# Hashed attention into a channel-mix layer: mu transposed in slot 5 of the first block, the third pair's turns and signs a slot down, natural loads ahead of the signs

## The chip, the cores and the metric

The kernel runs on one core of one Trainium2 chip. The metric is the time of one execution on the device in microseconds (us), the median over several runs. The engines are named as in the profile: PE is TensorE (matmul), PEld its weight load, DVE is VectorE, ACT is ScalarE, POOL is GpSimd, SP is SyncE, which issues most of the transfers; an engine's name with a q behind it (SPq, POOLq) is its queue of issues.

## The reference

The first half is attention in 32 heads (4 batches of 8, 768 tokens, 64 dimensions), in which a query sees only the keys of its own hash bucket. The bucket of a row is the six signs of its product with `proj`. The second half is a channel mix per batch: the attention output `x` is blended with itself shifted by one token, with the weights `mu_k` and `mu_r`, and goes through three matrices.

```python
q_bits = (np.einsum('bhsd,dk->bhsk', q, proj) > 0)      # k_bits likewise; proj is 64 x 6
mask = q_bucket[:, :, :, None] == k_bucket[:, :, None, :]
scores = np.where(mask, scale * np.matmul(q, k.transpose(0, 1, 3, 2)), -1e9)
attn_out = softmax(scores) @ v
...
xk = mu_k * x + (1.0 - mu_k) * x_prev                    # x: 4 x 768 x 512
xr = mu_r * x + (1.0 - mu_r) * x_prev
k = np.maximum(xk @ w_k, 0.0)                            # w_k: 512 x 1024
v = k * k @ w_v                                          # w_v: 1024 x 512
r = 1.0 / (1.0 + np.exp(-(xr @ w_r)))                    # w_r: 512 x 512
out = r * v
```

## The kernel before

The heads are taken two at a time, as 16 pairs `n` = 0 to 15, four to a batch. A pair has two heads `j` with six chunks of keys `jc` each, so twelve slots `s` = 0 to 11; slots are counted through as `G` = 12 n + s. The order in each engine's queue is written out by hand: the loop at L742 emits, slot by slot, everything that any engine does, and each engine works through its own queue in that order. Waits between engines follow from the data and from the buffers.

**A slot.** `score` (L445) makes one tile of scores, two matmuls of 70 rows: 64 dimensions and six signs. The signs are stored as plus and minus one half, so that a key of another bucket falls behind by a whole step, and ScalarE's exponential (L458, 128x768) turns that into nothing. Two score tiles can stand at a time. `pv` (L466) multiplies the exponentials of two slots earlier with the values; with the last chunk of a head VectorE takes the reciprocal and scales the output (L489, L490).

**Preparing a pair.** The operands `aq`, `ak` of a pair come out of four steps that are done during the pairs before it:
- `load_v` and `load_qk` (or, from pair 6 on, `load_blocks`) put the loads on SP's queue; `load_qk(n)` is two transfers of 384 KB and `load_v(n)` one. The line at L748 sets the slot.
- `turn(n, i, j, which, casts)` (L311) transposes q (i = 0) or k (i = 1) of head j in three fp32 transposes into a PSUM bank; VectorE copies that bank to SBUF (L330 for q, L332 for k), and two casts to bf16 bring its halves into `aq` or `ak` (L336, L337). The casts are done by GpSimd and VectorE, or both by GpSimd where `pool2` is given. The copied tiles `tq`, `tk` have one buffer each, a half for each head, and the next pair's go into the same.
- `bits(n, js, which)` (L403) multiplies the copied tiles with `projp` into a bank, VectorE takes the signs (`sg`, L413), and SP carries them into rows 64 to 69 of `aq` and `ak`: two small transfers (L418) per side and head, eight for a whole pair, the first head's ahead of the second's. `bits_direct` (L391) does the same for pair 0 without transfers.
- `values(n, j)` (L423) casts the values on GpSimd and adds them up over the chunks (two memsets, a cast, three additions).

**Behind a pair.** `turn_out(n)` (L497) transposes the output of a pair into a bank, VectorE copies it to `xt` (L504), and a shifted copy within `xt` (L508, L509) is made by GpSimd, or by VectorE in the fourth pair of a batch. `mix` (L514) needs the whole of `xt`: step 0 is the difference `df` (L521), step 1 the product with `mu_sb` (L525), step 2 the sum (L535), all on VectorE.

**Banks.** Besides the two score tiles there are four PSUM banks, A to D. In the first block (pairs 0 to 3) A and C collect the attention output of the two heads, and B and D serve all turns, signs, `turn_out` and the transposed mu; `misc_bank` gives B or D by slot. A bank is free again when VectorE has copied what stood in it.

**Mu.** `mu_k` and `mu_r` are loaded as eight rows (L698, L701), behind the loads of pairs 0 to 2 on SP's queue. TensorE transposes them into bank B and VectorE copies that to `mu_sb` (L770, L771), in slot 13; the first `mix` step that reads it stands in slot 19.

The order of the first 13 slots is the table `first_block` (L708). From pair 1 on general rules hold: signs of pair n+1 in slot 2, turns of pair n+2 in slots 4, 6, 8, 10, values of pair n+1 in slots 6 and 9 of the first block. The weights of the mix layer are loaded on GpSimd's queue in the slots of the table `weights` (L723). From pair 4 on the matmuls of the mix layer run between the attention slots, a share of them in every slot (`ffn`), with what is left behind pair 15.

Of the kernel before, what the change touches and what calls it, by code (L numbers as in the profile page):

```python
# [9 lines left out]
FP32 = mybir.dt.float32  # L10
# [6 lines left out]
P = 128  # L17
# [14 lines left out]
def kernel(  # L32
# [13 lines left out]
    nc = tc.nc  # L46
    B, H, S, D = q.shape
# [5 lines left out]
    NDC = DM // P  # L53
    NFC = DF // P
    NPB = H // 2
# [5 lines left out]
    ident32 = consts.tile([P, P], FP32, name="ident32")  # L61
# [13 lines left out]
    mu_rows = consts.tile([2 * NDC, P], FP32, name="mu_rows")  # L75
    mu_sb = consts.tile([P, 2 * NDC], FP32, name="mu_sb")
# [96 lines left out]
    def fast():  # L173
        with ExitStack() as fx:
# [4 lines left out]
            NKEEP = NPB + 2  # L179
# [21 lines left out]
            def bank(which, shape, dt, name):  # L201
                return bkp.tile(shape, dt, name=name, tag=f"bk{which}")
# [32 lines left out]
            def run_due():  # L235
                ready = sorted(x[:2] for x in due if x[0] <= clock[0])
                for key in ready:
                    fn = next(x for x in due if x[:2] == key)
                    due.remove(fn)
                    fn[2]()  # L240
# [70 lines left out]
            def turn(n, i, j, which, casts=None, copy=None):  # L311

                side = "qk"[i]
                au = augs[n % NSET]
                tp = bank(which, [P, HALF], FP32, f"tp{side}{n}_{j}")
                for c in range(3):
                    cols = slice(c * P, (c + 1) * P)
                    nc.tensor.transpose(tp[:, cols], nats[n][:, i, j, cols], ident32)  # L318
                if j == 0:
                    turned[n, side] = turnp.tile([P, S], FP32, name=f"t{side}{n}", tag=f"t{side}")  # L320
                dst = turned[n, side][:, j * HALF : (j + 1) * HALF]
                t32s[n, side, j] = dst
                if copy:
                    scale = 1.0 if side == "q" else ALPHA
                    nc.scalar.activation(dst, tp, AF.Copy, scale=scale)
                    nc.gpsimd.tensor_copy(au[side, j][0:D, 0:HALF], dst[0:D, :])
                    nc.scalar.activation(au[side, j][0:D, HALF:S], tp[D:P, :], AF.Copy, scale=scale)
                    return
                if side == "q":
                    nc.vector.tensor_copy(dst, tp)  # L330
                else:
                    nc.vector.tensor_scalar(  # L332
                        out=dst, in0=tp, scalar1=ALPHA, scalar2=None, op0=ALU.mult
                    )
                e0, e1 = casts or (nc.gpsimd, nc.vector)
                e0.tensor_copy(au[side, j][0:D, 0:HALF], dst[0:D, :])  # L336
                e1.tensor_copy(au[side, j][0:D, HALF:S], dst[D:P, :])  # L337
# [53 lines left out]
            def bits_direct(n, i, j, which):  # L391

                side = "qk"[i]
                bb = bank(which, [P, HALF], FP32, f"bd{side}{n}_{j}")
                nc.tensor.matmul(bb, projd, t32s[n, side, j], start=True, stop=True)
                for e in range(2):
                    nc.vector.tensor_scalar(
                        out=augs[n % NSET][side, j][D:AUG, e * HALF : (e + 1) * HALF],
                        in0=bb[D + 32 * e : D + 32 * e + NB, :],
                        scalar1=0.0, scalar2=0.5, op0=ALU.is_gt, op1=ALU.subtract,  # L400
                    )
# [285 lines left out]
            pool2 = (nc.gpsimd, nc.gpsimd)  # L687
            turn(0, 0, 0, "B", pool2)
            turn(0, 1, 0, "D", copy=True)
            for dst in (  # L690
# [13 lines left out]
            values(0, 0)  # L704
            turn(0, 0, 1, "B", pool2)
            turn(0, 1, 1, "D", pool2)

            first_block = {  # L708
                1: [lambda: bits_direct(0, 0, 1, "C")],
                2: [lambda: bits_direct(0, 1, 1, "B")],  # L710
                3: [lambda: turn(1, 0, 0, "D", pool2)],
                4: [lambda: turn(1, 1, 0, "C", pool2)],
                6: [lambda: bits(1, (0,), "B"), lambda: turn(1, 0, 1, "D")],
                8: [lambda: turn(1, 1, 1, "B")],
                9: [lambda: bits(1, (1,), "D"), lambda: turn(2, 0, 0, "B")],
                10: [lambda: turn(2, 1, 0, "D")],
                11: [lambda: turn(2, 0, 1, "B")],
                12: [lambda: turn(2, 1, 1, "D")],
            }


# [1 line left out]
            weights = {  # L723
                0: {10: ("k", 0, 2)},
                1: {6: ("k", 2, 2), 11: ("r", 0, 2)},
                2: {5: ("r", 2, 2), 9: ("v", 0, 4)},
                3: {2: ("v", 4, 4)},
            }
            LAG = 2
            MIXSLOT = 6  # L730
# [5 lines left out]
            def oo_bank(n, j):  # L736
                return "AC"[j] if n < NPB else "AB"[j]
# [4 lines left out]
            for G in range(nslots + LAG):  # L742
                clock[0] = G
                n, s = divmod(G, 12)
                live = G < nslots
                run_due()

                if live and s == (1 if n == 0 or n > NPB else 6 if n == NPB - 1 else 3):  # L748
                    if n < NPAIRS - 2:
                        load_v(n + 2)  # L750
                    if n + 3 < NPAIRS:
                        (load_qk if n + 3 < NKEEP else load_blocks)(n + 3)
                w = weights.get(n, {}).get(s)
                if w:
                    load_w(*w)
                old = chunks[G - LAG] if G >= LAG else None
                first = old is not None and old[2] == 0
                if live:
                    score(*chunks[G])
                if old and not first:  # L760
                    pv(*old, oo_bank(*old[:2]))
                rate = 25.9 / (NPB * 12 + (3 if n >= NPAIRS - NPB else 0))
                ffn(rate / 2)
                mb = misc_bank(n, s)
                if live:
                    for x in first_block.get(G, ()):
                        x()
                    if n == 1 and s == 1:
                        mups = bank("B", [P, 2 * NDC], FP32, "mups")
                        nc.tensor.transpose(mups, mu_rows, ident32[0 : 2 * NDC, 0 : 2 * NDC])  # L770
                        nc.vector.tensor_copy(mu_sb, mups)  # L771

                    if s == 2 and 1 <= n < NKEEP - 1:
                        bits(n + 1, (0, 1), "B")
                    if s == 10 and NKEEP <= n + 2 < NPAIRS:
                        bits_blocks(n + 2, "A")
                    if s == 3 and n >= 1:
                        turn_out(n - 1, mb)
                    if n >= NPB:
                        if s == 4 and n % NPB == 0:  # L780
                            mix((n - 1) // NPB, (n - 1) % NPB, 0)

                        if s in (8, 9) and n % NPB:
                            mix((n - 1) // NPB, (n - 1) % NPB, 0, [(0,), (1, 2)][s - 8])
                    ms = (5, 7, 9)
                    if s in ms and 1 <= n < NPB:
                        mix(0, n - 1, 0, [ms.index(s)])

                    xs = [NPB * 12 + x for x in (5, 10, 11, 12)]
                    if G in xs:  # L790
                        mix(0, xs.index(G), 1)
                    if n > NPB and s == (10 if n % NPB else 5):
                        mix((n - 1) // NPB, (n - 1) % NPB, 1)
                    if s in (4, 6, 8, 10) and 1 <= n < NKEEP - 2:
                        x = (s - 4) // 2
                        turn(n + 2, x % 2, x // 2, mb)
                    ts = (6, 7) if n % NPB == 0 else (4, 5)
                    if s in ts and NKEEP <= n + 2 < NPAIRS:
                        turn_blocks(n + 2, ts.index(s))
                    if n == 0 and s == 1:  # L800
                        values(0, 1)
                    vs_ = (8, 10) if n == 0 else (6, 9) if n < NPB else (0, 2)
                    if s in vs_ and n + 1 < NPAIRS:
                        values(n + 1, vs_.index(s))
                    if s in (8, 10) and NKEEP <= n + 2 < NPAIRS:
                        norm(n + 2, (s - 8) // 2)
                ffn(rate / 2)
                if old and first:
                    pv(*old, oo_bank(*old[:2]))
                if live and n >= NPB and n % NPB == 0 and s == MIXSLOT - 1:  # L810
                    queue.extend(ffn_items(n // NPB - 1))
# [14 lines left out]
            G = nslots + LAG  # L826
# [19 lines left out]
            x = 0  # L846
# [178 lines left out]
```

## Time and profile before

| | |
|---|---|
| median of 3 runs (lowest, highest) | 269.08 us (268.41, 269.61) |
| profiled execution: time, span | 269.2 us, 267.3 us |
| mean granted TensorE clock | 0.989 |
| busy: PE, ACT, DVE, POOL | 250.1, 216.0, 183.0, 121.2 us |
| ScalarE's exponentials, L458 | 192 of 909 ns, 167.4 us |
| ScalarE idle ahead of them | 24.1 us, 22.1 of it for scores |
| start of the scores of slots 14, 26, 38 | 22.99, 37.03, 47.55 us |

The span goes from the first to the last instruction; 1.9 us of the execution lie outside it. The 192 exponentials are one per slot. The profile's instructions carry the line of `kernel.py`, so the same line stands for all pairs; which pair an instruction belongs to is told from its order in time.

### The profile page before, as it was taken

Reading aid. Unit: us, or ns where it says so; the run is one execution under the profiler, and the core shown is the slowest. Engines: PE = TensorE matmul, PEld = TensorE weight load, DVE = VectorE, ACT = ScalarE, POOL = GpSimd, SP = SyncE. Lnnn points to the kernel's source line nnn. Section 1 sums busy time; section 2 is a strip of 40 time slices with the busy share of each in tenths; the row PEclk is TensorE's granted clock in tenths of the full one; section 3 lists DMA queues with packets and bytes.
Section 4 is the critical chain, followed back from the end, with each engine's and each line's share of the span. In section 5 each row is a group of like instructions: output and inputs, shape, how many; then the busy total and the mean of one; then the engine's idle time right before and its main releaser. Section 6 shows DMA issues by size and latency. Waiting matters only on the chain.

```text
span 267.3 us, 6634 instructions
## 1 busy us (share of the span) xinstructions
PE 250.1 (94%) x2441; PEld 151.6 (57%) x2441; DVE 183.0 (68%) x381; ACT 216.0 (81%) x320; POOL 121.2 (45%) x247
## 2 busy tenths in 40 slices
PE   7897999799999999999999999998999999989990
PEld 5564767465555655555565656564656665545450
DVE  2868578577899684759679586868596645775440
ACT  3576789888999998988999998989999988179700
POOL 3778478676768181822756293705483000000000
PEclk9999899999999999999999999999999999999998
DMA  7915195997769193977847291959520002220042
GB/s 227 369 57 83 14 259 98 237 207 160 170 122 241 36 221 63 205 195 192 209 127 155 63 214 22 234 173 242 146 60 6 3 2 82 78 78 0 14 151 86
DMA packets 26488, 35.41 MB, mean 132 GB/s; under 512 B 3064, under 2 KB 22992, under 8 KB 26448
## 3 DMA queue, kind: packets, MB, share of 16 engines
q1 hardware_dynamic: 23936, 31.89, 46.3%
q0 software_dynamic: 2144, 2.62, 6.4%
q8 instruction: 21, 0.34, 0.6%
q10 hardware_dynamic: 368, 0.39, 0.5%
q14 instruction: 19, 0.16, 0.2%
HBM read 30.68 MB, written 6.29 MB: 138 GB/s over the span
## 4 chain that ended last, share of the span: by engine, by line
PE 70%; DVE 10%; ACT 8%; DMA 5%; issue 2%; POOL 1%; SPq 0%; ACTq 0%; DVEq 0%
PE sc L451 16%; PE vp L553 15%; PE kp L553 12%; PE oo L478 9%; PE rp L553 7%; ACT pt L458 6%; DMA qk<-in_k_dram 3%; PE bb L369 2%; PE ot L503 2%; PE oo L469 2%; PE bb L409 2%; DMA vf<-in_v_dram 1%; DMA qk<-in_q_dram 1%; ACT sq L303 1%; PE tpq L318 1%
## 5 line engine op out<-in xcount | busy, mean ns | idle before, releaser
L458 ACT ACTIVATE pt<-sc,expb 128x768 bf16<-128x768 f32 x192 | 167.4, 909 | 24.1 <-PE sc L451 22.1
L451 PE MATMUL sc<-aq,ak 70*128 70x384 bf16 x384 | 94.5, 327 | 1.8 <-ACT pt L458 0.5
L478 PEld LDWEIGHTS <-pt 128*128 128x128 bf16 x1152 | 61.0, 98 | 26.8 <-issue 1.1
L478 PE MATMUL oo<-va,pt 128*128 128x65 bf16 x1152 | 66.9, 194 | 0.0
L553 PE MATMUL kp<-xk,wk_sb 128*128 128x384 bf16 x256 | 55.7, 326 | 2.6 <-DVE kr L578 1.1
L553 PE MATMUL vp<-wv_sb,k 128*128 128x512 bf16 (+1 forms) x200 | 51.9, 371 | 0.0
L451 PEld LDWEIGHTS <-ak 70*128 70x128 bf16 x384 | 35.2, 98 | 26.2 <-issue 5.1
L586 DVE TENSOR_TENSOR k<-kr 128x384 bf16<-128x384 bf16 x64 | 26.7, 433 | 6.4 <-ACT kr L576 5.9
L553 PEld LDWEIGHTS <-wk_sb 128*128 128x128 bf16 x256 | 21.7, 97 | 14.2 <-issue 4.0
L553 PE MATMUL rp<-wr_sb,xr 128*128 128x512 bf16 x96 | 28.9, 379 | 0.1
L353 POOL CAST aq<-tq 64x768 bf16<-64x768 f32 x20 | 16.5, 823 | 26.6 <-PE sc L451 11.9
L509 POOL COPY xt<-xt 128x127 bf16<-128x127 bf16 x12 | 3.5, 293 | 48.5 <-DVE xt L504 48.5
L576 ACT ACTIVATE kr<-kp 128x384 bf16<-128x384 f32 x36 | 18.1, 503 | 7.8 <-PE kp L553 7.8
L553 PEld LDWEIGHTS <-k 128*128 128x128 bf16 x200 | 16.8, 97 | 12.8 <-issue 2.7
L439 POOL TENSOR_TENSOR s<-vf 128x192 f32<-128x192 f32 x32 | 22.0, 688 | 0.0
L618 DVE SCALAR_TENSOR_TENSOR os<-th,vp 128x512 f32<-128x512 bf16 (+1 forms) x25 | 16.5, 662 | 7.2 <-PE vp L553 6.0
L489 DVE RECIPROCAL rc<-oo 128x6 f32<-128x6 f32 x32 | 6.1, 190 | 21.8 <-PE oo L478 21.8
L504 DVE COPY xt<-ot 128x768 bf16<-128x768 bf16 x16 | 8.9, 558 | 17.2 <-PE ot L503 17.0
L578 DVE TENSOR_SCALAR kr<-kp 128x384 bf16<-128x384 f32 x28 | 15.4, 552 | 6.9 <-PE kp L553 6.6
L490 DVE TENSOR_TENSOR ob<-oo,rc 128x384 bf16<-128x384 f32 x32 | 17.8, 558 | 1.1
L355 POOL TENSOR_SCALAR ak<-tk 64x768 bf16<-64x768 f32 x20 | 16.6, 832 | 2.8 <-DVE tk L343 1.3
L303 ACT ACTIVATE sq<-blk 128x768 bf16<-128x768 f32 x20 | 17.1, 853 | 0.0
(83 smaller groups left out, 305.8 us busy)
## 6 DMA issues: line engine op xcount, KB each, us to landing
blk<-in_q_dram SPq DMA_DIRECT2D x40, 176.0 KB
blk<-in_k_dram SPq DMA_DIRECT2D x40, 176.0 KB
vf<-in_v_dram SPq DMA_DIRECT2D x16, 384.0 KB
out_dram<-os SPq DMA_DIRECT2D x23, 256.0 KB
qk<-in_q_dram SPq DMA_DIRECT2D x5, 384.0 KB
qk<-in_k_dram SPq DMA_DIRECT2D x5, 384.0 KB
wk_sb<-in_moe_w_k_dram POOLq DMA_DIRECT2D x2, 512.0 KB, 5.6
wv_sb<-in_moe_w_v_dram POOLq DMA_DIRECT2D x2, 512.0 KB, 8.8
```

Source lines behind the costliest of these rows:

```text
L303: nc.scalar.activation(junk.rearrange("p (u d) -> p u d", u=NTOK), blks[n][:, i, :, 0:32], AF.Square, scale=1.5, accum_out=nrm[:, i, n : n ...
L353: eng.tensor_copy(dst, src)
L355: eng.tensor_scalar(out=dst, in0=src, scalar1=ALPHA, scalar2=1.0, op0=ALU.mult, op1=ALU.mult,)
L439: nc.gpsimd.tensor_add(s3, vf[:, 0 : 3 * D], vf[:, 3 * D : 6 * D])
L451: nc.tensor.matmul(sc[:, sp, 0:HALF], au["k", j][:, jc * P : (jc + 1) * P], au["q", j][:, sp * HALF : (sp + 1) * HALF], start=True, stop=True,
L458: nc.scalar.activation(pt.rearrange("p (s q) -> p s q", s=2), sc[:, :, 0:HALF], AF.Exp, bias=expb, scale=SCALE,)
L478: nc.tensor.matmul(oo[:, ic, :], pts[n, j, jc][:, ic * P : (ic + 1) * P], vas[n, j][:, jc, :], start=False, stop=(jc == NC_ - 1 and ic == ...
L490: nc.vector.tensor_tensor(out=obs[n][:, :, j * D : (j + 1) * D], in0=oo[:, :, 0:D], in1=rc.to_broadcast([P, NC_, D]), op=ALU.mult,)
L553: nc.tensor.matmul(box["t"], lhs(), rhs(), start=(i == 0), stop=(i == len(mms) - 1))
L576: nc.scalar.activation(kr, kp, AF.Relu, scale=HALFROOT)
L586: lambda: nc.vector.tensor_tensor(out=k2, in0=kr, in1=kr, op=ALU.mult),
L618: nc.vector.scalar_tensor_tensor(out=os_, in0=mx["th", b, c][:, ms], scalar=1.0, in1=vp, op0=ALU.add, op1=ALU.mult,)
```

## The change

- The transposed mu moves from slot 13 to slot 5, still in bank B.
- In block 0 no slot has two entries any more: the turn of pair 1's second q goes from slot 6 to 7, and the four turns of pair 2 from slots 9 to 12 to slots 10 to 13. Their casts, one of two on VectorE before, are both done by GpSimd.
- The signs of pair 2 go from slot 14 to 15, and the turns of pair 3 from slots 16, 18, 20, 22 to slots 17, 19, 21, 23, in the same banks as before. (The text's "third pair" is pair 2.)
- The natural loads of pairs 1 and 2 (`load_v` of pairs 3 and 4, `load_qk` of pairs 4 and 5) go from slot 3 of the pair to slot 1, on SP's queue ahead of that pair's eight sign transfers and not behind them.
- The second half of `w_r` is loaded in slot 4 of pair 2, not 5, and the second half of `w_v` in slot 0 of pair 3, not 2.

```diff
+            def transpose_mu():
+                mups = bank("B", [P, 2 * NDC], FP32, "mups")
+                nc.tensor.transpose(mups, mu_rows, ident32[0 : 2 * NDC, 0 : 2 * NDC])
+                nc.vector.tensor_copy(mu_sb, mups)
             first_block = {
...
-                6: [lambda: bits(1, (0,), "B"), lambda: turn(1, 0, 1, "D")],
-                8: [lambda: turn(1, 1, 1, "B")],
-                9: [lambda: bits(1, (1,), "D"), lambda: turn(2, 0, 0, "B")],
-                10: [lambda: turn(2, 1, 0, "D")],
-                11: [lambda: turn(2, 0, 1, "B")],
-                12: [lambda: turn(2, 1, 1, "D")],
...
+                5: transpose_mu,
+                6: lambda: bits(1, (0,), "B"),
+                7: lambda: turn(1, 0, 1, "D"),
+                8: lambda: turn(1, 1, 1, "B"),
+                9: lambda: bits(1, (1,), "D"),
+                10: lambda: turn(2, 0, 0, "B", pool2),
+                11: lambda: turn(2, 1, 0, "D", pool2),
+                12: lambda: turn(2, 0, 1, "B", pool2),
+                13: lambda: turn(2, 1, 1, "D", pool2),
             }
...
-                2: {5: ("r", 2, 2), 9: ("v", 0, 4)},
-                3: {2: ("v", 4, 4)},
+                2: {4: ("r", 2, 2), 9: ("v", 0, 4)},
+                3: {0: ("v", 4, 4)},
...
-                if live and s == (1 if n == 0 or n > NPB else 6 if n == NPB - 1 else 3):
+                if live and s == (6 if n == NPB - 1 else 3 if n == NPB else 1):
                     if n < NPAIRS - 2:
                         load_v(n + 2)
                     if n + 3 < NPAIRS:
...
-                    if n == 1 and s == 1:
-                        mups = bank("B", [P, 2 * NDC], FP32, "mups")
-                        nc.tensor.transpose(mups, mu_rows, ident32[0 : 2 * NDC, 0 : 2 * NDC])
-                        nc.vector.tensor_copy(mu_sb, mups)
-
-                    if s == 2 and 1 <= n < NKEEP - 1:
+                    if s == (3 if n == 1 else 2) and 1 <= n < NKEEP - 1:
                         bits(n + 1, (0, 1), "B")
...
-                    if s in (4, 6, 8, 10) and 1 <= n < NKEEP - 2:
-                        x = (s - 4) // 2
+                    tn = (5, 7, 9, 11) if n == 1 else (4, 6, 8, 10)
+                    if s in tn and 1 <= n < NKEEP - 2:
+                        x = tn.index(s)
                         turn(n + 2, x % 2, x // 2, mb)
```

More of the change, by code (lines that the diff above doesn't have):

```diff
@@ L706, in fast @@
             turn(0, 1, 1, "D", pool2)
+            def transpose_mu():
+                mups = bank("B", [P, 2 * NDC], FP32, "mups")
+                nc.tensor.transpose(mups, mu_rows, ident32[0 : 2 * NDC, 0 : 2 * NDC])
+                nc.vector.tensor_copy(mu_sb, mups)
             first_block = {
[L709 to L712, printed above, removed]
-                6: [lambda: bits(1, (0,), "B"), lambda: turn(1, 0, 1, "D")],
-                8: [lambda: turn(1, 1, 1, "B")],
-                9: [lambda: bits(1, (1,), "D"), lambda: turn(2, 0, 0, "B")],
-                10: [lambda: turn(2, 1, 0, "D")],
-                11: [lambda: turn(2, 0, 1, "B")],
-                12: [lambda: turn(2, 1, 1, "D")],
+                1: lambda: bits_direct(0, 0, 1, "C"),
+                2: lambda: bits_direct(0, 1, 1, "B"),
+                3: lambda: turn(1, 0, 0, "D", pool2),
+                4: lambda: turn(1, 1, 0, "C", pool2),
+                5: transpose_mu,
[7 more added lines that the diff above has]
+                13: lambda: turn(2, 1, 1, "D", pool2),
             }
@@ L765, in fast @@
                 if live:
-                    for x in first_block.get(G, ()):
-                        x()
-                    if n == 1 and s == 1:
-                        mups = bank("B", [P, 2 * NDC], FP32, "mups")
-                        nc.tensor.transpose(mups, mu_rows, ident32[0 : 2 * NDC, 0 : 2 * NDC])
-                        nc.vector.tensor_copy(mu_sb, mups)
-                    if s == 2 and 1 <= n < NKEEP - 1:
+                    if G in first_block:
+                        first_block[G]()
+                    if s == (3 if n == 1 else 2) and 1 <= n < NKEEP - 1:
                         bits(n + 1, (0, 1), "B")
```

## The prediction, made before the result was known

> **What bounds the kernel now.** I read the page first (ScalarE 81% busy, TensorE 94%, and a chain that is 70% TensorE over the whole span), then ScalarE's row of the timeline over the first five pairs of heads, where the diff works. A slot is one score tile and one 128x768 exponential, so every gap in this row is lost time. The columns are start, duration, engine and line, operation, count, and in brackets the idle time before.
>
> ```profile
> 12.51 3.44 ACT L458 ACTIVATE pt<-sc,expb 128x768 bf16<-128x768 f32 x4 [0.42 <-PE sc L451]
> 16.68 2.48 ACT L458 ACTIVATE pt<-sc,expb 128x768 bf16<-128x768 f32 x3 [0.73 <-PE sc L451]
> 20.20 4.30 ACT L458 ACTIVATE pt<-sc,expb 128x768 bf16<-128x768 f32 x5 [1.04 <-PE sc L451]
> 27.81 0.90 ACT L458 ACTIVATE pt<-sc,expb 128x768 bf16<-128x768 f32 x1 [3.31 <-PE sc L451]
> 29.43 9.13 ACT L458 ACTIVATE pt<-sc,expb 128x768 bf16<-128x768 f32 x11 [0.71 <-PE sc L451]
> 39.17 9.90 ACT L458 ACTIVATE pt<-sc,expb 128x768 bf16<-128x768 f32 x12 [0.62 <-PE sc L451]
> 49.69 3.41 ACT L458 ACTIVATE pt<-sc,expb 128x768 bf16<-128x768 f32 x4 [0.62 <-PE sc L451]
> 54.56 6.47 ACT L458 ACTIVATE pt<-sc,expb 128x768 bf16<-128x768 f32 x8 [1.46 <-PE sc L451]
> ```
>
> Between the gaps ScalarE never rests: 9.13 us for 11 tiles is 0.83 us a slot. In slots 6 to 42 the gaps sum to 0.73 + 1.04 + 3.31 + 0.71 + 0.62 + 0.62 + 1.46 = 8.49 us. Two are large. For the first I read the timeline of VectorE and TensorE.
>
> ```profile
> 22.30 1.37 DVE L337 CAST aq<-tq 64x384 bf16<-64x384 f32 x1
> ...
> 25.14 0.16 DVE L771 COPY mu_sb<-mups 128x8 f32<-128x8 f32 x1
> ...
> 25.35 0.51 PE L409 MATMUL bb<-tq,projp 128*32 128x384 f32 x1 [1.86 <-DVE mu_sb L771]
> ```
>
> The transposed mu (22.83, slot 13) sits in bank B until VectorE copies it out at 25.14, and VectorE is late: it still has copies and casts of pair 2 to do, one of them stretched from 0.35 to 1.37 us beside GpSimd's work. The sign products of pair 2 (slot 14) want bank B, so TensorE stands. The wait is paid twice: in the windows of 1 us the granted clock (the column after the five engines) falls to half behind it.
>
> ```profile
> 25.00:26.00 1.00, 0.65 (x8) 0.16 (x8) 0.29 (x2) 0.00 (x0) 1.00 (x4) 0.98 1.14 212
> 26.00:27.00 1.00, 1.00 (x12) 0.59 (x9) 0.56 (x1) 0.00 (x0) 0.03 (x1) 0.50 0.49 90
> 27.00:28.00 1.00, 1.00 (x12) 0.65 (x10) 0.00 (x0) 0.19 (x1) 0.00 (x0) 0.50 0.00 0
> ```
>
> The second large gap is in the chain of waits: pair 5's k, issued behind eight sign transfers, lands at 53.48, and its transpose waits 1.45 us.
>
> ```profile
> 45.89 7.59 DMA qk<-in_k_dram
> 53.48 0.14 issue
> 53.61 0.52 PE tpk L318 x3
> ```
>
> **The change, part by part.** The sum is made against the profiled execution: 269.2 us, its span of 267.3 and 1.9 around it; the median, 269.08, is 0.1 lower.
>
> Mu in slot 5. It adds a 0.22 us transpose and a 0.16 us copy there and removes both from slot 13. TensorE gets to it at 14.40. Ahead of the mu loads on SP's queue stand eight loads of 384 KB, 3.15 MB; the rates of the 1 us windows sum to 3.1 MB by 11.0, and even the loads behind mu are through by 14.3. So mu is there; were it not, the wait would be about 1 us at most. Behind the transpose stand the score of slot 6 and the sign products in B, which wait for a copy that ends near 14.9 and start at 15.07 instead of 15.01: nothing lost. In slot 6 the 0.48 us turn no longer stands between the signs and the score of slot 7, so the gap of 0.73 becomes about 0.35.
>
> Turns of pairs 1 and 2 a slot down. In slot 9 the sign products wait for the k copy of slot 8. VectorE now runs q copy and cast behind reciprocal and product of the last output (0.22 + 0.48 + 0.58 + 0.30 from 16.5, k copy to 18.65), so the products end near 19.6 rather than 19.30, but the turn of 0.48 behind them is gone. The score of slot 10 comes at 19.95 rather than 20.11. With ScalarE's queue emptied at 18.80, that gap is 1.25 instead of 1.04, and its next tile starts at 20.05.
>
> Casts on GpSimd. VectorE loses four casts (0.42, 0.41, 1.37, 0.35 us) in slots 9 to 13, GpSimd gains four at 0.55 (14.02, 14.57, 15.14: start to start). So VectorE keeps up: the turns of slots 10 to 13 then cost TensorE 0.35 beside 0.51 for score and output, hidden under 0.83. The k copy of slot 13 ends near 24.15; the sign products of slot 15 start near 24.5 with nothing in their way. The 3.31 is gone. But products (0.78) and output transposes (0.35) now share slot 15, so the score of slot 16 comes near 25.7 and the 0.71 stays as about 0.75. That tile starts at 26.1 instead of 29.43: 3.3 us gained here (5.79 of gaps become 2.35).
>
> GpSimd's queue is the price. Before, it had 3.32 us to spare:
>
> ```profile
> 25.49 0.50 POOL L336 CAST ak<-tk 64x384 bf16<-64x384 f32 x1
> 25.94 0.09 POOL L508 MEMSET xt<- 128x1 bf16 x1
> 29.35 0.29 POOL L509 COPY xt<-xt 128x127 bf16<-128x127 bf16 x1 [3.32 <-DVE xt L504]
> ```
>
> After, from the second cast of pair 1 done at 19.4: value sums 1.87, weight issue 0.94, casts 1.1, value sums 1.9, six casts 3.3, set and copy 0.4, so the shifted copy of the first output tile ends at 28.8, where VectorE writes that tile at 26.3. The mix difference (L521), now in slot 17 ahead of the turn in VectorE's queue, waits until 28.85, 2 us behind its slot. From there to the last k copy of pair 3 VectorE needs the 5.4 us it took from 31.03 to 36.43, and one q copy and cast more (0.95), which stood ahead of the difference before: 35.0 or so. The sign products of slot 26 would start at 34.0 and now at 34.8 to 35.0. The gap there grows from 0.62 to about 1.4: 0.8 lost. That is my least sure term: 0 if GpSimd runs 0.8 sooner, 1.6 if 0.8 later. I take 0.8, the sum of its rows. Value sums of pair 2 end near 33.7, ahead of their use at 35.6.
>
> Loads ahead of the signs. In pairs 1 and 2 the loads move from slot 3 to slot 1, past eight sign issues of 0.68. Pair 5's k then goes out near 34.5 instead of 45.89, and the turn that waited for it comes near 50: the 1.46 goes, and ScalarE, full up to 53.10, has nothing else late there. What the signs pay, by the nearest rows: pair 4's 1.18 MB, issued 32.64 to 34.20 with a weight load of as much time beside it, was through by 39.5, the windows show. The same load from 23.3 is through by 28.5; the first head's four signs, issued 25.4 to 28.1, land near 30, and slot 24 wants them at 32. In pair 2: issued to 38.6, wanted near 43.9. Nothing, from below; the bound from above is a rival.
>
> Weights. Two GpSimd issues (0.71 and 0.78) a slot or two sooner pass one cast that waits for VectorE anyway; hidden in idle times of 1.36 and 0.65 there.
>
> Sum: 3.3 (rounded down from 5.79 - 2.35 = 3.4) - 0.8 + 1.5 = 4.0; 269.2 - 4.0 = 265.2, and 0.1 less for the median: 265.1. Behind 62 us nothing moves in slots, and every later stage starts sooner by the same.
>
> **The rivals.** One: the queue costs nothing. The difference also waits less if GpSimd's value sums run undisturbed, and 0.8 comes back: 264.3; were slot 10's gap of 1.25 to vanish as well, 263.0. For it: VectorE makes fewer casts against GpSimd. Against: the sum above is of undisturbed rows already.
>
> Two: the loads bring little. Weight loads near 40 to 50 us may hold up something else, and the 1.46 stays: 266.6. Against it are the 11 us by which the load goes out sooner.
>
> Three: GpSimd is later still. Its casts take 0.69 to 0.74 beside a cast on VectorE, not 0.50. If the stretch to 28.8 grows by 2 us, TensorE waits 2.8 before slot 26 and the clock halves again, as it did after 1.86: 2 for the wait and about 0.7 for the gap behind it, 267.8. The trace bears this price out: 1.86 us of wait gave the clock of 0.50, 1.45 us at 53.6 did not. The Trainium skill (TensorE: Matmul & The Clock Gate, Part 1) has the clock fall only after an idle window of about 3.4 us; by that rule 0.7 falls away, but the trace halved it after less.
>
> Four, on the slower side: the signs starve behind the loads. A sign transfer put on SP's queue after 1.18 MB lands with the rest of it. Where the loads drain as slowly as pair 5's k did (7.59 us from issue, with weight loads beside it), signs issued at 28.1 land at 35.7 and slot 24 waits 3.6; in slot 36 (38.6 + 7.6 = 46.2 against 43.9) 2.3 more. With 0.7 for the clock twice that is 7.3 against a gain of 4.0: 272.4. It begins to cost when a sign takes over 4 us to land, and makes the kernel slower when both together pass 4.0. Against it: a weight load ran beside pair 4's load too, and 5.2 us sufficed for both. The Trainium skill (DMA: Bandwidth & Descriptors, Queues, rings and completion order) says that each DMA engine takes one queue's descriptors in ring order and changes between queues by packets. By that rule signs do wait for the loads, and its time would be that of this rival if weights took half the engines; no row of before shows a sign behind a load.
>
> That the change does not act as said hardly can be: the wait of slot 14 is one on bank B.
>
> **How the numbers follow.** Forecast 0.50 (264.3 to 266.3); rival one 0.19, two 0.12, three 0.12, four 0.07. A measurement of this kernel can tell about 0.5%, 1.35 us, from no change. Forecast, one and two are faster, and half of three: 0.87; the other half, near 267.8 and above, is the same: 0.06; four is slower: 0.07. The range from 262.9 to 268.3 leaves out rival four, the worst of three, and a little below.
>
> **What would show it.** Right: no ScalarE gap over 1.5 us from 12 to 60 us, clock 1.00 throughout, the eleventh tile of pair 1 no later than 33 us, a GpSimd xt copy near 28.8 with VectorE's L521 waiting for it, no wait for qk in pair 3. Wrong: a wait of scores for aq or ak from a DMA at slots 24 or 36 (rival four), a TensorE wait over 1.8 us for VectorE at slot 26 (three), a wait for mu_rows in slot 5.

## The result and the profile after

The changed kernel takes 266.39 us (median of 6 runs, 265.33 to 266.69), the kernel before in the same session 268.75 (6 runs): a ratio of 0.9903, 95% interval 0.9875 to 0.9931, so 2.6 us faster (0.0097 of 268.75; 1.9 to 3.4); the two medians differ by 2.4. The forecast was 265.1. In the table of the experiments the ratios leave out runs that lie over 1.5% above the fastest of their kernel and the medians do not, which matters for one kernel there, loads_back. The profiled execution took 266.43 with a span of 264.6, against 269.2 and 267.3 before.

ScalarE's row of the timeline, for the stretch shown of before:

```profile
13.63 3.48 ACT L458 ACTIVATE pt<-sc,expb 128x768 bf16<-128x768 f32 x4 [0.42 <-PE sc L451]
17.58 2.78 ACT L458 ACTIVATE pt<-sc,expb 128x768 bf16<-128x768 f32 x3 [0.48 <-PE sc L451]
21.23 5.17 ACT L458 ACTIVATE pt<-sc,expb 128x768 bf16<-128x768 f32 x6 [0.87 <-PE sc L451]
27.13 6.64 ACT L458 ACTIVATE pt<-sc,expb 128x768 bf16<-128x768 f32 x8 [0.72 <-PE sc L451]
34.14 2.48 ACT L458 ACTIVATE pt<-sc,expb 128x768 bf16<-128x768 f32 x3 [0.38 <-PE sc L451]
37.59 9.90 ACT L458 ACTIVATE pt<-sc,expb 128x768 bf16<-128x768 f32 x12 [0.97 <-PE sc L451]
48.11 9.90 ACT L458 ACTIVATE pt<-sc,expb 128x768 bf16<-128x768 f32 x12 [0.62 <-PE sc L451]
```

The 3.31 and the 1.46 are gone: ahead of slots 7 to 43 the gaps sum to 0.48 + 0.87 + 0.72 + 0.38 + 0.97 + 0.62 = 4.04 us against 8.49. A gap of 0.38 ahead of slot 24 is new, and the 0.62 ahead of slot 27 has become 0.97. What the forecast named as the cause stands in VectorE's row and in GpSimd's, and the run xt_vector below tests it:

```profile
26.83 0.55 DVE L504 COPY xt<-ot 128x768 bf16<-128x768 bf16 x1
30.02 0.56 DVE L521 TENSOR_TENSOR df<-xt 128x768 bf16<-128x768 bf16 x1 [2.64 <-POOL xt L509]
```

```profile
29.09 0.50 POOL L337 CAST ak<-tk 64x384 bf16<-64x384 f32 x1
29.54 0.10 POOL L508 MEMSET xt<- 128x1 bf16 x1
29.70 0.29 POOL L509 COPY xt<-xt 128x127 bf16<-128x127 bf16 x1
```

Where GpSimd waited 3.32 us for the output tile before, VectorE now waits 2.64 us for GpSimd. And everything stands about 1.1 us late against the working of the forecast. There are 4.4 us fewer gaps, but the span is only 2.7 us shorter: of the difference 1.1 went ahead of the first tile, 0.3 behind the last one, and the rest within the stretches between the gaps. Two pieces of the chain of waits (start, duration, what), of before and of after:

```profile
6.04 0.90 PE bdq L395 x2
```

```profile
6.30 1.62 PE bdq L395 x2
7.92 1.29 PE bdk L395 x2
```

The same two products take 0.90 and 1.62 us. The trace's record of the granted clock begins with full clock at 5.48 us before and at 9.44 after; the first tile starts at 9.38 and 10.46. The stream of instructions up to there is the same in both.

### The profile page after: what moved, and what is told of

It reads as the page before. It is cut to its first block, busy times and chain, and to the rows that moved or that the text cites. A ratio compares the mean times of both kernels' runs of the same rounds, so it can differ in the third digit from the quotient of the medians.

```text
span 264.6 us, 6633 instructions
## 1 busy us (share of the span) xinstructions
PE 250.3 (95%) x2441; PEld 151.5 (57%) x2441; DVE 180.0 (68%) x377; ACT 216.1 (82%) x320; POOL 123.0 (46%) x251
## 4 chain that ended last, share of the span: by engine, by line
PE 72%; ACT 9%; DVE 7%; POOL 4%; DMA 2%; issue 2%; SPq 0%; ACTq 0%; DVEq 0%; POOLq 0%
PE sc L451 17%; PE vp L553 15%; PE kp L553 14%; PE oo L478 9%; ACT pt L458 8%; PE rp L553 7%; PE bb L369 3%; PE oo L469 2%; PE ot L503 2%; PE bb L409 1%; DMA vf<-in_v_dram 1%; DMA qk<-in_q_dram 1%; PE bdq L395 1%; DVE ob L490 1%; DVE kr L578 1%
## 5 line engine op out<-in xcount | busy, mean ns | idle before, releaser
L553 PE MATMUL rp<-wr_sb,xr 128*128 128x512 bf16 x96 | 28.9, 379 | 0.1
L439 POOL TENSOR_TENSOR s<-vf 128x192 f32<-128x192 f32 x32 | 22.7, 708 | 0.0
```

Of the source, the lines that this page charges most:

```text
L439: nc.gpsimd.tensor_add(s3, vf[:, 0 : 3 * D], vf[:, 3 * D : 6 * D])
L553: nc.tensor.matmul(box["t"], lhs(), rhs(), start=(i == 0), stop=(i == len(mms) - 1))
```

## The experiments

To keep the start apart from the rest, I read the start of each slot's tile in ScalarE's row, take it from the first tile of the same execution, and subtract the same difference of the kernel before. So -3.38 in column "slot 16" means that the work from slot 0 to slot 16 took 3.38 us less than before. One execution of each kernel was profiled. The first six columns of numbers are of that execution, the median is of the timed runs. In the same comparisons the kernel before had medians of 268.75 (changed), 269.21 (the next four kernels of the table), 268.77 (the next three, and before_again) and 269.50 (the last three).

| kernel | full clock at | first tile | slot 16 | slot 28 | slot 44 | last tile | median us | ratio to before (95%) |
|---|---|---|---|---|---|---|---|---|
| before | 5.48 | 9.38 | 0 | 0 | 0 | 0 | 268.75 | |
| before_again | 9.66 | 10.43 | 0.01 | -0.07 | -1.20 | -1.15 | 269.11 (one) | |
| changed | 9.44 | 10.46 | -3.38 | -2.66 | -4.25 | -4.02 | 266.39 | 0.9903 (0.9875 to 0.9931) |
| loads_alone | 4.42 | 9.32 | +0.59 | +1.30 | -0.27 | 0.00 | 268.82 | 0.9976 (0.9951 to 1.0001) |
| mu_alone | 10.23 | 10.77 | -2.84 | -2.91 | -4.01 | -4.18 | 266.31 | 0.9899 (0.9862 to 0.9935) |
| split_casts | 9.39 | 10.35 | -2.11 | -2.36 | -3.94 | -3.61 | 266.06 | 0.9884 (0.9852 to 0.9916) |
| xt_vector | 4.60 | 9.39 | -3.38 | -3.52 | -5.10 | -4.72 | 265.02 | 0.9855 (0.9823 to 0.9887) |
| loads_back | 9.46 | 10.30 | -3.45 | -2.72 | -3.19 | -2.99 | 267.27 | 0.9924 (0.9890 to 0.9957) |
| fill | 5.61 | 9.68 | -3.39 | -2.67 | -4.25 | -3.89 | 265.86 | 0.9886 (0.9856 to 0.9916) |
| fill_xt | 3.86 | 9.22 | -3.38 | -3.51 | -5.09 | -3.72 | 264.73 | 0.9847 (0.9815 to 0.9878) |
| late_wv | 5.34 | 9.44 | -3.38 | -2.65 | -4.24 | +1.54 | 271.47 | 1.0100 (1.0050 to 1.0151) |
| spread | 4.33 | 9.23 | -3.72 | -3.53 | -5.12 | -4.84 | 264.62 | 0.9834 (0.9798 to 0.9869) |
| no_warm | 10.47 | 10.77 | -3.74 | -2.97 | -4.55 | -4.16 | 266.21 (one) | |

**mu_alone: the kernel before, with mu transposed in slot 5 and nothing else.**

```diff
+                5: [lambda: transpose_mu()],
...
-                    if n == 1 and s == 1:
-                        mups = bank("B", [P, 2 * NDC], FP32, "mups")
-                        nc.tensor.transpose(mups, mu_rows, ident32[0 : 2 * NDC, 0 : 2 * NDC])
-                        nc.vector.tensor_copy(mu_sb, mups)
```

> The kernel before with only the transposed mu moved to slot 5; turns, casts, signs and loads as before. Queue theory: bank B is free, but the sign products of pair 2 still wait for the k copy that VectorE ends at 24.13, so they start there and not at 25.35, and the clock stays full: about 2.0 us less than before (1.6 to 2.4), a wait of TensorE for L332 or L337 in place of L771. Rival, the bank alone: the whole 3.3 us. Rival, VectorE's lateness alone: under 0.5 us.

Measured: the chip gives 2.84 by slot 16, more than the queue theory had. ScalarE's gap, and TensorE's wait in its place (who waited for whom: total, times, longest):

```profile
27.14 9.91 ACT L458 ACTIVATE pt<-sc,expb 128x768 bf16<-128x768 f32 x12 [1.40 <-PE sc L451]
51.95 6.47 ACT L458 ACTIVATE pt<-sc,expb 128x768 bf16<-128x768 f32 x8 [0.36 <-PE sc L451]
```

```profile
PEld bb L409 <- DVE tk L332: 0.7, 1, 0.7
```

The wait for L332 instead of L771 is as expected, but it is 0.7 us, and the clock stays full, which my 2.0 had not counted in whole. Slot 14's scores start 0.24 us sooner, and from there to the output behind the sign products it takes 1.20 less (2.05 against 3.25); so 1.4 of the 2.84 comes behind the wait. The kernel before ran 3.41 us at half clock there, which is up to 1.7 us of work lost. Moving mu gives the whole of the change's measured gain; the turns, casts and loads together add nothing that the times can tell (266.31 and 266.39). The second line was not foreseen either: pair 5's k, loaded in slot 3 as before, is waited for 0.36 us here, not 1.46.

**loads_alone: the kernel before, with the loads and the two weight issues moved.**

```diff
-                if live and s == (1 if n == 0 or n > NPB else 6 if n == NPB - 1 else 3):
+                if live and s == (6 if n == NPB - 1 else 3 if n == NPB else 1):
...
-                2: {5: ("r", 2, 2), 9: ("v", 0, 4)},
-                3: {2: ("v", 4, 4)},
+                2: {4: ("r", 2, 2), 9: ("v", 0, 4)},
+                3: {0: ("v", 4, 4)},
```

> The kernel before with only the loads (slot 1 of pairs 1 and 2, ahead of the signs) and the two weight issues moved. Queue theory (each gap of ScalarE has its own cause): the wait for pair 5's k goes and nothing else, so about 1.5 us less than before (1.2 to 1.7), and the 3.31 us gap at slot 15 stays. Rival, signs behind the loads: waits for aq or ak ahead of slots 24 and 36, up to 5.8 us, slower than before. Rival, another transfer takes the place: no gain.

Measured: between slots 40 and 44 it gains 1.58 us, as expected against that execution. But by slot 18 it had lost 1.3, behind a wait for mu no longer than before (1.87 us). ScalarE's row there:

```profile
28.34 0.90 ACT L458 ACTIVATE pt<-sc,expb 128x768 bf16<-128x768 f32 x1 [3.87 <-PE sc L451]
29.96 0.90 ACT L458 ACTIVATE pt<-sc,expb 128x768 bf16<-128x768 f32 x1 [0.71 <-PE sc L451]
31.62 8.19 ACT L458 ACTIVATE pt<-sc,expb 128x768 bf16<-128x768 f32 x10 [0.76 <-PE sc L451]
```

The clock's record shows why: half speed for 6.83 us from 24.91, where the kernel before had 3.41 from 25.96; another 3.4 us at half clock are up to 1.7 us of work lost. No tile of slots 24 or 36 waits for signs. The median is 0.4 below that of the kernel before in the same runs (269.21), not 1.5, and the interval just touches no change.

**before_again: the kernel before, for a second profile.**

> The kernel before once more, for a second profile. Theory: the wait for mu at slot 14 is there again with the clock halved behind it for 3.4 or 6.8 us; the start of the first tile (9.38 before) and the wait for pair 5's k (1.45 before) differ from run to run by up to 1 us each. If they are fixed, both are as before within 0.1.

ScalarE's row, at the wait for mu and at the wait for pair 5's k:

```profile
29.00 0.90 ACT L458 ACTIVATE pt<-sc,expb 128x768 bf16<-128x768 f32 x1 [3.53 <-PE sc L451]
30.49 9.05 ACT L458 ACTIVATE pt<-sc,expb 128x768 bf16<-128x768 f32 x11 [0.58 <-PE sc L451]
...
54.41 6.47 ACT L458 ACTIVATE pt<-sc,expb 128x768 bf16<-128x768 f32 x8 [0.33 <-PE sc L451]
```

The wait for mu costs the same (3.53 + 0.58 against 3.31 + 0.71). The other two do not repeat: the wait for k costs 0.33 and not 1.46, and the first tile starts at 10.43 and not 9.38. So the two profiles of the first comparison are mixtures: that of the kernel before has an early start and a long wait for k, that of the changed kernel a late start. The span of both profiles of before is 267.3, because in each the two differences cancel.

**loads_back: the changed kernel with the loads in slot 3 again** (the changed condition in the diff of loads_alone undone; the two weight issues stay where the change put them).

> The changed kernel with the loads of pairs 1 and 2 in slot 3 again, behind the signs; all else as changed. As forecast (the wait for pair 5's k is 1.46 us): 1.5 us slower than the changed kernel. Revised after the runs with one part alone (its landing took 7.59 us from issue in one execution, 6.49 in another, so the wait differs from run to run): 0.4 us slower (0.1 to 0.8), and a gap of ScalarE of 0.3 to 1.5 us near slot 43. If the loads' place costs the signs something: faster.

ScalarE's row, near slot 43:

```profile
52.30 6.47 ACT L458 ACTIVATE pt<-sc,expb 128x768 bf16<-128x768 f32 x8 [0.99 <-PE sc L451]
```

The wait for k is back with 0.99, inside the revised 0.3 to 1.5, and slot 44 is 1.06 later than in the changed kernel. By the ratios (0.9924, and 0.9886 for `fill` in the same runs) the difference is about 1 us with intervals that overlap, so the times alone don't settle 0.4 against 1.5. Four executions with the loads in slot 3 (before, before_again, mu_alone, loads_back) waited 1.46, 0.33, 0.36 and 0.99: 0.8 on average. What makes them differ was not found.

**late_wv: loads_back with w_v loaded later.**

```diff
-                2: {4: ("r", 2, 2), 9: ("v", 0, 4)},
-                3: {0: ("v", 4, 4)},
+                2: {4: ("r", 2, 2)},
+                3: {8: ("v", 0, 4), 11: ("v", 4, 4)},
```

> The changed kernel with the loads of pairs 1 and 2 in slot 3 again, and w_v loaded in slots 8 and 11 of pair 3, not from slot 9 of pair 2 on. Theory: pair 5's k lands late only because the two loads of w_v take half of the transfer time beside it; without them the 1.18 MB land some 4 us after issue, ScalarE's gap near slot 43 (0.99 us with the loads in slot 3) is gone, and slot 44 stands as with the loads in slot 1: 0.4 to 1.0 us less than with the loads in slot 3. Rival, the eight signs ahead on SP's queue are the cause: the gap stays.

At slot 44 it stands at -4.24, as with the loads in slot 1: without w_v beside it, k is there in time with eight signs still ahead of it on SP's queue. So the signs ahead of it do not make k late by themselves. Nor do the weights: with the loads in slot 1, as in the changed kernel, w_v is loaded as early and k is not waited for. It takes both, loads issued late and weights beside them, and removing either is enough. The expected gain did not come, though: the weights now run beside the loads of pair 6, and a transfer of those takes 11.36 us in the chain of waits,

```profile
57.28 11.36 DMA blk<-in_k_dram
68.77 0.99 DVE tk L343
```

which loses more than 5 us between slots 54 and 66. TensorE stands for 3.37 us there, and the clock, full until then, is at half for 3.41 us from 70.19. The wait was moved, and grew.

**split_casts: the changed kernel, with the turns of pair 2 casting half on VectorE again** (`pool2` left out in slots 10 to 13).

> The changed kernel with the four turns of pair 2 casting half on VectorE again. Queue theory: GpSimd's shifted copy of the first output ends some 2 us sooner and the 0.8 us lost between slots 20 and 28 comes back; but VectorE has 2.5 us of casts more against 1.0 us of idle time, so the sign products of slot 15 wait about 1 us. Together 0.3 us slower than the changed kernel (0.3 less to 0.8 more). Rival, the casts on GpSimd only cost: 0.8 less. Rival, VectorE's casts beside GpSimd were the main wait: 2 us more, and the clock halved.

ScalarE's row from slot 16 on:

```profile
28.29 8.88 ACT L458 ACTIVATE pt<-sc,expb 128x768 bf16<-128x768 f32 x11 [1.99 <-PE sc L451]
37.79 9.91 ACT L458 ACTIVATE pt<-sc,expb 128x768 bf16<-128x768 f32 x12 [0.61 <-PE sc L451]
```

As the queue theory has it: slot 16 loses 1.27 against the changed kernel, the losses ahead of slots 24 and 27 are gone, and at the end it is 0.4 later (0.3 expected). The medians (266.06 and 266.39) cannot tell that from nothing.

**xt_vector: the changed kernel, with the first output's shifted copy on VectorE.**

```diff
-                eng = nc.vector if t == NPB - 1 else nc.gpsimd
+                eng = nc.vector if t == NPB - 1 or n == 0 else nc.gpsimd
```

> The changed kernel with the first output's set and shifted copy (L508, L509 for pair 0) on VectorE, so that L521 does not stand behind GpSimd's casts. Queue theory: L521 starts near its slot, 2 us sooner, the sign products of slot 26 no longer wait for VectorE, and the 0.8 us lost between slots 20 and 28 comes back: 0.8 us less than the changed kernel (0.5 to 1.0). Rival, something else on GpSimd (value sums of pair 2, casts) sets slot 26: no gain.

Measured, the mix difference of pair 0:

```profile
26.57 0.75 DVE L521 TENSOR_TENSOR df<-xt 128x768 bf16<-128x768 bf16 x1
```

That is VectorE's row. L521 starts 17.2 us behind the first tile, where it was 19.6 in the changed kernel, and waits for nothing. Of the 0.72 lost between slots 16 and 28 all is back (-3.52 at slot 28), 0.7 at the end. So GpSimd's queue, through that one copy, was the loss. The median, 265.02, is 1.4 below the changed kernel's, in another session; the profile shows 0.7 of that, and what the rest is was not found.

**fill and no_warm: the start.** `fill` adds idle products to the changed kernel, `no_warm` takes away 20 of the 22 (the loop runs to 2) and adds none; `fill_xt` is fill with the copy on VectorE.

```diff
-            for _ in range(22):
+            for _ in range(26):
...
             turn(0, 1, 0, "D", copy=True)
+            for _ in range(6):
+                nc.tensor.matmul(idle, epsm, epsm, start=True, stop=True)
```

> The changed kernel with ten more idle products at the start (26 instead of 22 ahead of the first turn, six more ahead of the first signs), so that TensorE has no gap before 6.3 us. Theory: how soon the clock is full (4.4 to 10.2 us in the six profiles so far) sets the first tile (9.3 to 10.8 us); without gaps the clock is full by 8, the first tile starts by 9.7, and the median is 0.5 us below the changed kernel (0.2 to 1.0). Rival, the landing of the first loads sets the start: no gain, or 0.2 us lost to the added products.

> The changed kernel with 2 instead of 22 idle products at the start. If the clock sets the start: full not before 7 us (7 to 10.5), the first tile at 10.3 to 11.0 us. If the landing of the first loads sets it: 9.4 to 10.4 as in the others, whatever the clock.

> Both edits: the ten idle products and the first output's shifted copy on VectorE. If the two are independent: 0.5 us less than the run with the copy on VectorE alone, 264.5 (264.0 to 265.0), some 4.5 us below the kernel before.

In no_warm the q load landed at 3.71, as early as in the kernel before (3.70), and in the chain of waits the two products of the start take

```profile
6.05 1.62 PE bdq L395 x2
7.67 1.28 PE bdk L395 x2
```

with the clock full at 10.47 and the first tile at 10.77: the clock sets the start, not the landing. Over all 13 profiles the first tile is at 9.22 to 9.68 where the clock was full by 5.61, and at 10.30 to 10.77 where it was full from 9.39 on; nothing lies between. The three profiles with the added products (fill, fill_xt, and spread below) have an early clock, but so have four of the nine with the 22 products of before, so that the added ones bring it about is likely and not shown. The medians are 0.5 and 0.3 below those without (changed and xt_vector), inside the spread. That fill_xt has -3.72 at its last tile comes from one loss of 0.8 near 121 us, where VectorE waits 2.2 us for an output transfer; no other profile has it.

**spread: fill_xt, with the first output's transposes in slot 16.**

```diff
-                    if s == 3 and n >= 1:
-                        turn_out(n - 1, mb)
+                    if s == (4 if n == 1 else 3) and n >= 1:
+                        turn_out(n - 1, "D" if n == 1 else mb)
```

> The changed kernel with the idle products and the first shifted copy on VectorE, and the first output's transposes in slot 16, bank D, so that slot 15 holds the sign products alone. Queue theory: the gap of 0.72 ahead of slot 16 falls to about 0.4, as products alone; 0.3 us less than without (0 to 0.5), near 264.4. Rival, VectorE gets the output later and the loss comes back ahead of slot 28: no gain.

ScalarE's row, ahead of slots 16 and 27:

```profile
25.57 9.12 ACT L458 ACTIVATE pt<-sc,expb 128x768 bf16<-128x768 f32 x11 [0.39 <-PE sc L451]
35.50 9.90 ACT L458 ACTIVATE pt<-sc,expb 128x768 bf16<-128x768 f32 x12 [0.81 <-PE sc L451]
```

The gap ahead of slot 16 falls to 0.39 as expected, and by slot 28 the gain is gone (-3.53, -3.51 without): the rival. With 264.62 and 0.9834 it is, beside fill_xt, the fastest of the runs; the two are not told apart.

## Why the prediction was right, and where it was not

**The wait for mu (3.3 forecast).** It gave 3.38 by slot 16, and nothing waited for `mu_rows` in slot 5. Its parts were not as I had them: I ascribed the gain to bank B and the relieved VectorE together, and the move of mu alone gives 2.84 of it, turns and casts the other 0.54.

**Gaps of slots 7 and 10.** They came as 0.48 and 0.87, against 0.35 and 1.25 forecast: the second got smaller (1.04 before), not larger. That is less of a gain than it looks, since the three tiles between them take 2.78 us and not 2.48; that the sum up to slot 16 still came out owes something to luck.

**GpSimd's queue (0.8).** The step least sure in the sum came out best in size: 0.72 is lost between slots 16 and 28, and xt_vector brings it back. The copy ends at 29.99. Its rows in the forecast add up to 28.9 (28.8 is written there), and this execution started 1.1 late. VectorE's part was reckoned less well. The forecast's own terms (28.85, 5.4 and 0.95) make 35.2, not 35.0, and the last k copy of pair 3 ends at 35.82, which is 34.7 without the late start. And the loss was forecast ahead of slot 27 alone, but half of it stands ahead of slot 24, where a transpose waits 0.43 us for VectorE's k copy. By the profile split_casts ends 0.4 later, so there the price was worth paying, if barely; the times can't tell.

**The loads (1.46).** This is the term that was mis-sized. Its mechanism holds (with the loads in slot 1 no execution waits for k), but I took from one profiled execution a wait that differs between executions: 0.33 to 1.46 in four. Against before_again the changed kernel's last tile is 2.9 us sooner (4.02 - 1.15), and against the first profile 4.0; the times say 2.6. With the mean of 0.8 in place of 1.46 and the 0.3 behind the last tile, the first profile would give 3.1, an estimate that lies inside the interval of 1.9 to 3.4. Rival two, which gave the loads nothing, named 266.6, nearest to what was measured, for a reason that did not occur; that was luck.

**The start (not in the sum).** 1.08 us of difference ahead of the first tile, out of the clock's state and not out of the change, had no place in the forecast. It explains the profiled span (4.02 - 1.08 = 2.9; 0.3 of that is lost behind the last tile). For the medians it should cancel if the timed runs of both kernels have early and late starts alike, which the times do not show.

**Rival three** had GpSimd 2 us later and the clock halved: no wait of TensorE behind slot 16 was long enough, and the clock is full from 9.44 to 262. Its price for a halved clock, 0.7, was low: mu_alone leaves 1.4 for it, and twice as long at half clock cost loads_alone 1.3 more.

**Rival four** had signs starve behind the loads: slots 24 and 36 wait for no transfer, with the signs of pair 2 issued from 26.94 to 33.6 behind loads of 24.20 to 25.61. But its mechanism is there. The trace's records of single packets, told apart by their size (768 bytes for signs, 1536 for loads), show the packets of the three loads from 27.22 to 31.29. (The forecast had them through by 28.5, 5.2 us from the first issue; its own row for pair 4's loads, 32.64 to 39.5, has 6.9, which makes 30.2, as measured without the late start.) Five sign transfers issued from 26.94 to 29.82, which take 0.7 us from one to the next, ran all together from 30.35 to 31.25, at the end of the loads. In late_wv, where the loads were through at 47.69, a sign issued at 51.41 ran at 52.71. So the first sign waited some 2 us for the loads; it cost nothing, because slot 24's scores start only at 33.56. The kernel before has such a case too, which the forecast had missed: a sign issued at 49.49 ran at 53.16, just behind the loads ahead of it, whose packets end at 53.05. The rule of the Trainium skill cited there (DMA: Bandwidth & Descriptors, Queues, rings and completion order), that a DMA engine takes one queue's descriptors in ring order, agrees with that. Its other half, that the engines go round the queues that have work, fits late_wv: the packets of the three loads issued with pair 5's k take 4.05 us with no weight load beside them, against 7.05 in the kernel before, where those of w_v run from 49.49 on.

**The signs named in advance.** No gap ahead of an exponential from 12 to 60 us is over 0.97, the eleventh tile of pair 1 starts at 32.08, L521 waits for GpSimd's copy, and nothing waits for `qk` in pair 3. The clock is full from 9.44 on, so throughout from 12 us.

## What to carry to other kernels

Before a bound of one execution goes into a sum, see whether it repeats: a wait for data that lands beside other transfers, and the start, each moved by 1 us between executions of the same kernel, as much as the effect in question. A copy that stands in a bank holds up whoever needs the bank next, by as much as the copying engine is behind; move it to where that engine has just caught up. When work is given to an idle engine, look for the short instruction at the end of its queue that another engine waits for, and give that one back.

## What the runs showed of the hardware

TensorE's clock fell to half after TensorE had stood for 1.86 us (before), 1.87 (before_again and loads_alone) and 3.37 (late_wv). It stayed there for 3.41 us, in loads_alone for 6.83. Waits of 0.7 us (mu_alone) and 1.45 us (before, from 52.16) did not halve it. Every stretch between two changes of the clock in these records is a multiple of 3.41 us (3.41, 6.83, 17.07, 20.48, 64.85). The Trainium skill (TensorE: Matmul & The Clock Gate, Part 1) gives the window as 3413 ns, free-running, and the halves of these traces are one and two such windows; that the clock falls after an idle window of about 3.4 us is not what they show, since less was enough.

With the bounds counted on in steps of 3.41 us from the recorded changes, the 1.87 us of loads_alone lie 1.45 ahead of a bound (24.91, where the clock fell) and 0.42 behind it, and the 1.45 us of before are parted at 53.26 into 1.10 and 0.35. So 1.45 us within one window were enough, and where a wait falls between the bounds may count as well as its length. How much is needed is not shown: near the end of no_warm TensorE stands for 1.52 us between 256.23 and 259.64, and the clock is still full behind it.

At the start the same instructions put the first tile 1 us sooner or later, with the clock (13 profiles, 9.22 to 9.68 and 10.30 to 10.77). And the packets of the three loads issued with pair 5's k (1.18 MB) took 4.05 us with no weight load beside them (late_wv) and 5.96 to 7.05 with two (before, before_again, mu_alone, loads_back).
